# Gated S5 and SiLU mixture on one core: C and three quarters of x turned by transposing transfers

## The chip, the cores and the metric

The kernel runs on one core of a Trainium2 chip. The core has a matrix engine (TensorE, in the profile PE, its weight loads PEld), VectorE (DVE), ScalarE (ACT), GpSimd (POOL) and SyncE (SP), which does nothing here but issue transfers. The engines run side by side, each through its own list of instructions in order, and wait for each other through semaphores. The metric is the device time of one execution in microseconds, the median of some runs.

## The reference

For 2048 tokens x of width 448, two branches are computed and mixed by a gate of each token:

```python
x = A_x
g = _sigmoid((x * gate_w).sum(-1, keepdims=True))
# a: a diagonal complex recurrence (S5) with 448 states
dt = jnp.exp(log_dt)
Lam_bar = jnp.exp(dt * Lam)
B_bar = ((Lam_bar - 1.0) / Lam)[:, None] * Bmat
Bu = jnp.einsum("bld,pd->blp", x + 0j, B_bar)
for t in range(L):
    h = Lam_bar[None, :] * h + Bu[:, t, :]
    hs.append(h)
a = 2.0 * jnp.einsum("blp,dp->bld", hseq, Cmat).real + x * Dskip[None, None, :]
# b: a dense layer pair, width 1792
b = silu(x @ w1) @ w2
out = g * a + (1 - g) * b
```

Inputs and output are bf16.

## The kernel before

The tokens are cut into four chunks of 512 (`tc` 0 to 3) and sixteen blocks of 128 (`tb` 0 to 15). Everything that TensorE contracts over the width 448 needs x with the width on the partitions: that is the tile `xT`, four column groups of 128 (`XCOL` gives where they begin; they overlap) for each chunk. The natural x, with tokens on the partitions, is the tile `xnat`; it is also where the sum of the branches is gathered (`Tb` is another name for it).

For each chunk the work is:

- `x_products` (line 711): the products of `xT` with w1 ("F" tiles, 14 for each chunk) and with the turned B (`BT`, "B" tiles, 7 for each chunk). They run as half-array products of 64 rows, two tiles abreast, in pairs with two PSUM banks. `evict` (line 670) takes a pair out: F tiles through Silu on ScalarE into `aT`, B tiles into `UG`. For chunk 0, `UDVE` lists the B pairs that VectorE evicts; the others go to ScalarE.
- `lanes` (line 754): VectorE rotates `UG` by cosines and sines, runs seven scans of 512 steps (line 784), rotates back and leaves the states in `H`. GpSimd's transfers cast the scan's result to bf16. The products on the way back are written to `PO`; the later half of them has the name `PO1`. Chunk follows chunk, since a scan starts from the end of the one before.
- `gates` (line 897): VectorE multiplies `xnat` by the gate weights into `xg` and by the skip weights in place; ScalarE sums, takes tanh and scales. For chunks after the first it runs after `Gf0`, the first scan of the lanes then under way.
- `ffn2` (line 816, tag G): the product of `aT` with w2; ScalarE scales it into `fe` and a GpSimd transfer adds it into `xnat`.
- `readout` (line 834, tag C): the product of `H` with the readout weights `CP`. The result is scaled and added either by VectorE (line 853, into `ot`, five buffers, then a store), or, for the blocks in `OUTA`, by ScalarE (line 848, into `ct`), an adding transfer of GpSimd (line 850) and a store from `xnat`.

Three things are turned besides. Chunk 0 of x is turned by TensorE at the start (`x0_transposes`). Chunks 1 to 3 are turned by `x_transposes` (line 526): 32 transposes of 64x64 on TensorE into two banks, then two copies into `xT`. B is turned by TensorE (`b_transposes`). C is loaded in its natural form into `Cnat` (a part of `H[2]`; GpSimd clears the rest of it at line 462), turned in 32x32 blocks by VectorE (`readout_columns`, line 870, four instructions into a part of `UG[2]`), and 16 transfers of SP move the blocks to their places in `CP` (line 876). `readout_weights` (line 879) then scales C into `CP` in place: for slots 0 to 2 two ScalarE and two VectorE instructions each, for slot 3, where the real and the imaginary part share the 128 partitions, two half-height ScalarE instructions and one of VectorE.

TensorE's order is the order in which the program adds its work. That of the other engines comes from a planner (`Plan`): each operation has a cost, a priority (a smaller number goes first) and what it reads and writes; the planner plays the run through and sorts by its starting times. The transfers of one queue have rising priorities as they are added (`nl`), so SP's queue keeps the order of the code unless a transfer has to wait. The order is fixed when the program is built: an operation that comes late in the run holds all that the planner put behind it on its engine. `Waits` turns reads and writes by name into semaphore waits. The scaling of C (`CTAT`) is held to 59 us of the plan's time.

The last lines of the body set TensorE's order: F and B of chunks 0 and 1; G of blocks 0 to 3; F of chunk 1, B of chunk 2; G 4 to 7; the rest of F of chunk 2, B of chunk 3, F of chunk 3; C 0 to 7; G 8 to 13; C 8 to 11; G 14 and 15; C 12 to 15.

Of the kernel before, what the change touches and what calls it, by code (L numbers as in the profile page):

```python
# [7 lines left out]
ALU = mybir.AluOpType  # L8
AF = mybir.ActivationFunctionType
# [20 lines left out]
XPRIO = {2: 15, 3: 20.2}  # L30
XBLK = ()
XBEH = {2: "PI_0", 3: "H0_0"}
UDVE = (0, 1, 4, 5, 6)
OUTA = tuple(range(4, 12))
PRMF = (1, 0)
PRMP = 9.7
CPRIO = 2.9
# [3 lines left out]
CBEH = ""  # L41
# [257 lines left out]
def bass_gated_mix__ssm_conv_s5__dense_activation_silu__prompt_kernel(nc, A_x, A_Lambda_re, A_Lambda_im, A_B_re, A_B_im, A_C_re, A_C_im,  # L299
               A_log_dt, A_Dskip, B_x, B_w1, B_w2, gate_w, out):  # L300
    with ExitStack() as ctx:
# [3 lines left out]
        def sb(name, shape, dtype):  # L305
            return E(nc.sbuf_tensor(name, list(shape), dtype))
# [15 lines left out]
        Cnat = H[2][:, :, :].rearrange("p s n -> p (s n)").rearrange("p (b l) -> p b l", b=4)  # L322
        cnn = [f"H2_{s}" for s in range(7)]
# [9 lines left out]
        ot = [sb(f"ot{k}", [128, D_MOD], BF16) for k in range(NOT)]  # L333
        ones = nc.const_aps.tensor(1.0, [128, 512], BF16)
# [53 lines left out]
        def act_cost(n, aps=0):  # L388
            return 0.17 + n * 0.000833 + 0.09 * aps
# [18 lines left out]
        def load(q, dst, src, name, nbytes, prio=None, after=()):  # L408
            nl[0] += 1
            prio = nl[0] if prio is None else prio  # L410
            P.add(q, lambda e: e.dma_start(dst, src), list(after), name.split(), 0.6 if q == "pool" else 0.5 if nbytes > 2000 else 0.35, prio, sem(), nbytes, tag="ld " + name)  # L411
# [36 lines left out]
        def load_xn(tc):
            load("sp", xnat[:, 4 * tc:4 * tc + 4, :],
                 x2[tc * CH:(tc + 1) * CH, :].rearrange("(b p) d -> p b d", p=128), f"xn{tc}", CH * 896)  # L450

        def load_C():

            n = 0
            for b0, b1, p in ((0, 3, 128), (3, 4, 64)):
                rows = lambda a: a[128 * b0:128 * b0 + p * (b1 - b0), :].rearrange("(b p) l -> p b l", p=p)
                for dst, src in (((0, 448), rows(A_C_re)), ((512, 896), rows(A_C_im[:, 0:384])), ((448, 512), rows(A_C_im[:, 384:448]))):
                    load("sp", Cnat[0:p, b0:b1, dst[0]:dst[1]], src, f"Cn{n}" + (" " + " ".join(cnn) if n == 0 else ""),
                         p * (b1 - b0) * max(300, 2 * (dst[1] - dst[0])), None, ["Cnz"] * b0)
                    n += 1  # L460

        POOL(lambda e: e.memset(Cnat[:, 3, :], 0.0), [], ["Cnz"], 0.9, 5)
        load_xn(1)
        load_C()
        load("sp", w2s[:, :, :], B_w2.rearrange("(fb p) d -> p fb d", p=128), "w2", F_FF * 896)
        load_xn(2)
# [55 lines left out]
        for tc in XBLK:  # L522
            xn_of[tc] = {q: [f"xT{tc}_{g}{m}" for g in range(4) for m in range(4)] for q in range(4)}
# [23 lines left out]

        def x_blocks(tc):


            X32 = (xT[:, 3, :, :] if tc == 2 else H[2][:, 0:4, :]).rearrange("p m (q b i) -> p m q b i", q=4, i=32)
            names = [f"XT{tc}2_{k}" for k in range(4)]
            held = cnn if tc == 3 else xn_of[3][0]
            xs = xnat[:, 4 * tc:4 * tc + 4, :]
            for k, (q0, q1, c, b0, b1) in enumerate(((0, 3, 0, 0, 2), (0, 3, 0, 2, 4), (3, 4, XCOL[3], 0, 2), (3, 4, XCOL[3], 2, 4))):
                n = q1 - q0
                src = xs[:, b0:b1, c:c + 128 * n].rearrange("p b (q m i) -> p b q m i", q=n, i=32)
                dst = X32.rearrange("p m q b i -> p b q m i")[:, b0:b1, q0:q1, :, :]
                DVE(lambda e, dst=dst, src=src: e.transpose(dst, src), [f"xn{tc}"] + names[0:k][0:1], [names[k]] + cnn * (tc == 3 and k == 0), 0.15 + 256 * n / 960, XPRIO[tc], "xTd")
            k = sem()  # L560
            for g in range(4):
                for m in range(4):
                    to = xT[32 * m:32 * m + 32, tc, :, :].rearrange("p q (b g i) -> p (q b) g i", b=4, i=32)[:, :, g, :]
                    P.add("sp", lambda e, to=to, g=g, m=m: e.dma_start(to, X32[32 * g:32 * g + 32, m, :, :, :].rearrange("p q b i -> p (q b) i")),
                          names + held, [f"xT{tc}_{g}{m}"], 0.68, 400, k, 150000, tag="xTm")
# [293 lines left out]
        ctn = [f"CT{g}{m}" for g in range(4) for m in range(4)]  # L859

        def readout_columns():

            C32 = UG[2][:, 0:NSLOT, :].rearrange("p s n -> p (s n)").rearrange("p (m t b i) -> p m t b i", m=4, b=4, i=32)
            names = [f"X32_{k}" for k in range(4)]
            held = [f"U2_{s}" for s in range(7)] + ["U2_3i"]
            turned = [f"BT{s}_{h}" for s in range(7) for h in range(2)]
            for b in range(4):
                src = Cnat[:, b, :].rearrange("p (t m i) -> p t m i", m=4, i=32)
                dst = C32.rearrange("p m t b i -> p b t m i")[:, b, :, :, :]
                DVE(lambda e, dst=dst, src=src: e.transpose(dst, src), [f"Cn{n}" for n in range(6)] + ["Cnz"] + [CBEH] * (CBEH != "") + cnn + turned, [names[b]],  # L870
                    0.15 + 896 / 960, CPRIO, "CTd")
            k = sem()
            for g in range(4):
                for m in range(4):
                    to = CP[32 * m:32 * m + 32, :, :].rearrange("p t (b g i) -> p (t b) g i", b=4, i=32)[:, :, g, :]
                    P.add("sp", lambda e, to=to, g=g, m=m: e.dma_start(to, C32[32 * g:32 * g + 32, m, :, :, :].rearrange("p t b i -> p (t b) i")),
                          names + held, [f"CT{g}{m}"], 0.75, 400, k, 300000, tag="CTm")

        def readout_weights(k):

            re, im = CP[:, k, 0:D_MOD], CP[:, 4 + k, 0:D_MOD] if k < 3 else None
            c, cn = ct[k % 2], f"ct{k % 2}"
            both = [cn + "a"]
            if k < 3:
                ACT(lambda e: e.activation(c[:, 0, :], im, AF.Copy, scale=sc2[:, k:k + 1]), ctn + ["sc2"], [cn + "a"], act_cost(448, 1), 8, "ct").at = CTAT
                ACT(lambda e: e.activation(c[:, 1, :], re, AF.Copy, scale=sc2[:, k:k + 1]), ctn + ["sc2"], [cn + "b"], act_cost(448, 1), 8, "ct").at = CTAT
                both.append(cn + "b")
            else:
                for a, b in ((slice(0, 64), slice(64, 128)), (slice(64, 128), slice(0, 64))):
                    ACT(lambda e, a=a, b=b: e.activation(c[a, 0, :], CP[b, 3, 0:D_MOD], AF.Copy, scale=sc2[b, 3:4]), ctn + ["sc2"], [cn + "a"], act_cost(448, 1), 8, "ct").at = CTAT  # L890
            DVE(lambda e: e.scalar_tensor_tensor(re, re, sc1[:, k:k + 1], c[:, 0, :], ALU.mult, ALU.add),
                ctn + ["sc1"] + both, [f"CP{k}"], 0.68, CPP, "CP")
            if k < 3:
                DVE(lambda e: e.scalar_tensor_tensor(im, im, nsc1[:, k:k + 1], c[:, 1, :], ALU.mult, ALU.add),
                    ctn + ["sc1"] + both, [f"CP{4 + k}"], 0.68, CPP, "CP")
# [20 lines left out]
        def xt(tc, who):  # L916
            return [lambda: x_transposes(tc, who)]
# [7 lines left out]
        def C(*tbs):  # L925
# [6 lines left out]
                   {PRMF: [parameters], (K - 2, 0): turn_b[:1], K - 2: turn_b[1:2], K - 1: turn_b[2:], XT1K: xt(1, XT1), 8: [lambda: lanes(0)] + [readout_columns] + [lambda tc=tc: x_blocks(tc) for tc in XBLK]}, [K - 2])  # L932
# [7 lines left out]
        x_products(F(1) + F(2, 0, 1) + B(2), {2: xt(2, "aa")} if 2 not in XBLK else {})  # L940
# [4 lines left out]
        x_products(F(2, 1) + B(3) + F(3), {1: xt(3, "aa") if 3 not in XBLK else [], 9: [lambda: gates(3)]})  # L945
# [40 lines left out]
```

## Time and profile before

| | |
|---|---|
| median of 3 runs | 140.45 us (140.28 to 141.47) |
| the profiled execution | 140.08 us, its span 138.3 us |
| granted TensorE clock | 0.998 |
| busy: PE | 134.7 us (97%) |
| busy: DVE | 119.3 us (86%) |
| busy: ACT | 96.2 us (70%) |
| busy: POOL | 46.4 us (34%) |
| read from memory | 7.11 MB |

All places and lengths come from the profiled execution, whose span begins with its first instruction; the time of a run has some 1.8 us around the span. A line of the order of time gives the start, the length, the engine, the line of the code, the operation, what it writes and reads, and in brackets how long the engine stood idle before it and what ended that. An engine's name with a q (SPq) is its queue of issues. An engine that is busy most of the time is not by that the bound: the chain of waits, followed back from the last instruction, says whose time the kernel takes.

### The profile page before, as it was taken

Reading aid. Unit: us, or ns where it says so; the run is one execution under the profiler, and the core shown is the slowest. Engines: PE = TensorE matmul, PEld = TensorE weight load, DVE = VectorE, ACT = ScalarE, POOL = GpSimd, SP = SyncE. Lnnn points to the kernel's source line nnn. Section 1 sums busy time; section 2 is a strip of 40 time slices with the busy share of each in tenths; the row PEclk is TensorE's granted clock in tenths of the full one; section 3 lists DMA queues with packets and bytes.
Section 4 is the critical chain, followed back from the end, with each engine's and each line's share of the span. In section 5 each row is a group of like instructions: output and inputs, shape, how many; then the busy total and the mean of one; then the engine's idle time right before and its main releaser. Section 6 shows DMA issues by size and latency. Waiting matters only on the chain.

```text
span 138.3 us, 2881 instructions
## 1 busy us (share of the span) xinstructions
PE 134.7 (97%) x1137; PEld 66.0 (48%) x1137; DVE 119.3 (86%) x160; ACT 96.2 (70%) x167; POOL 46.4 (34%) x81
## 2 busy tenths in 40 slices
PE   7999999999999999999999999999999999999991
PEld 2545454445545444455454444445555555555561
DVE  0319999999999999999999999999999999992053
ACT  3259895999647999998299999899643149752200
POOL 7433030300548603067360030724063404374310
PEclk9999999999999999999999999999999999999999
DMA  4999999477859920029654010475459421379542
GB/s 140 324 355 292 270 364 341 63 102 83 96 77 155 158 40 19 24 37 160 93 87 64 0 38 0 65 120 81 114 106 159 102 33 18 51 100 151 118 102 68
DMA packets 33220, 16.48 MB, mean 119 GB/s; under 512 B 17075, under 2 KB 33078, under 8 KB 33206
## 3 DMA queue, kind: packets, MB, share of 16 engines
q0 software_dynamic: 7216, 6.43, 31.6%
q1 hardware_dynamic: 25440, 9.51, 25.8%
q10 hardware_dynamic: 550, 0.36, 0.8%
q8 instruction: 9, 0.15, 0.4%
q14 instruction: 5, 0.04, 0.1%
HBM read 7.11 MB, written 1.84 MB: 65 GB/s over the span
## 4 chain that ended last, share of the span: by engine, by line
PE 96%; DVE 1%; issue 0%; DVEq 0%
PE ps L711 46%; PE ps L822 31%; PE ps L843 14%; PE ps L489 2%; DVE ot L853 1%; PE ps L536 1%; PE ps L504 1%; PE ps L651 1%; PE ps L490 0%; PE ps L583 0%; PE ps L723 0%; DVEq L293 0%
## 5 line engine op out<-in xcount | busy, mean ns | idle before, releaser
L711 PE MATMUL ps<-xT,w1s 64*128 64x512 bf16 x392 | 48.2, 376 | 0.0
L822 PE MATMUL ps<-w2s,aT 128*128 128x448 bf16 x224 | 43.0, 353 | 0.0
L681 ACT ACTIVATE aT<-ps 128x1024 bf16<-128x1024 f32 (+1 forms) x30 | 28.9, 977 | 10.2 <-PE ps L711 10.1
L822 PEld LDWEIGHTS ps<-w2s,aT 128*128 128x128 bf16 x224 | 21.8, 98 | 20.9 <-issue 0.8
L711 PEld LDWEIGHTS ps<-xT,w1s 64*128 64x128 bf16 x392 | 19.6, 94 | 22.5 <-issue 1.2
L711 PE MATMUL ps<-xT,BT 64*128 64x512 bf16 x196 | 25.8, 376 | 0.0
L784 DVE TENSOR_TENSOR_SCAN Gf<-rc,gin,H 128x512 f32<-128x512 f32 x21 | 25.4, 1265 | 0.1
L830 POOL DMA_DIRECT2D xnat<-fe x16 | 14.4, 922 | 31.2 <-ACT fe L828 23.0
L843 PE MATMUL ps<-CP,H 128*128 128x448 bf16 (+2 forms) x126 | 21.7, 332 | 0.0
L411 POOL DMA_DIRECT2D UG<-Gf x27 | 15.7, 660 | 15.7 <-DVE Gf L784 15.4
L828 ACT ACTIVATE fe<-ps,g 128x448 bf16<-128x448 f32 x16 | 9.9, 627 | 11.1 <-PE ps L822 8.1
L843 PEld LDWEIGHTS ps<-CP,H 128*128 128x128 bf16 x126 | 11.6, 98 | 10.0 <-DVE xnat L752 0.4
L711 PEld LDWEIGHTS ps<-xT,BT 64*128 64x128 bf16 x196 | 10.8, 94 | 11.2 <-DVE Gf L609 0.2
L752 DVE TENSOR_TENSOR H<-UG,COS 128x3584 bf16<-128x3584 bf16 (+2 forms) x9 | 16.1, 1810 | 0.0
L411 POOL DMA_DIRECT2D UG<-UG x8 | 4.5, 567 | 27.1 <-ACT UG L690 27.1
L690 ACT ACTIVATE UG<-ps 128x1024 bf16<-128x1024 f32 (+1 forms) x13 | 11.8, 936 | 0.5 <-PE ps L711 0.5
L853 DVE SCALAR_TENSOR_TENSOR ot<-ps,g,xnat 128x448 bf16<-128x448 f32 (+2 forms) x10 | 5.7, 584 | 7.5 <-issue 6.2
L913 ACT ACTIVATE xnat<-xnat,g 128x448 bf16<-128x448 bf16 x16 | 9.7, 663 | 0.1
L906 ACT ACTIVATE junk<-xg 128x448 bf16<-128x448 bf16 x16 | 9.6, 598 | 0.1
L850 POOL DMA_DIRECT2D xnat<-ct x8 | 6.9, 864 | 6.7 <-ACT ct L848 6.6
L848 ACT ACTIVATE ct<-ps,g 128x448 f32<-128x448 f32 x8 | 5.1, 633 | 5.7 <-PE ps L843 5.7
L752 DVE TENSOR_TENSOR PI<-UG,SIN 128x1536 bf16<-128x1536 bf16 (+1 forms) x8 | 8.5, 1083 | 0.0
(99 smaller groups left out, 123.8 us busy)
## 6 DMA issues: line engine op xcount, KB each, us to landing
UG<-Gf POOLq DMA_DIRECT2D x21, 128.0 KB, 2.8
xnat<-fe POOLq DMA_DIRECT2D x16, 112.0 KB, 2.6
w2s<-in_B_w_dram SPq DMA_DIRECT2D x1, 1568.0 KB, 8.5
xnat<-in_A_x_dram SPq DMA_DIRECT2D x3, 448.0 KB, 8.2
CP<-UG SPq DMA_DIRECT2D x16, 56.0 KB, 2.4
xnat<-ct POOLq DMA_DIRECT2D x8, 112.0 KB, 2.9
out_dram<-xnat SPq DMA_DIRECT2D x8, 112.0 KB, 2.3
out_dram<-ot SPq DMA_DIRECT2D x7, 112.0 KB, 1.8
```

What stands on the lines that cost most here:

```text
L411: P.add(q, lambda e: e.dma_start(dst, src), list(after), name.split(), 0.6 if q == "pool" else 0.5 if nbytes > 2000 else 0.35, prio, sem() ...
L681: ACT(lambda e, src=src, dst=dst: e.activation(dst, src(), AF.Silu), [tk, "tbl"], [f"aT{tc % 2}_{m}" for m in names], act_cost(512 * n), 2 ...
L690: ACT(lambda e, src=src, dst=dst: e.activation(dst, src(), AF.Copy), [tk], after, act_cost(512 * n), 5, "U")
L711: r = pe.matmul(bk(toks[k], b), weights(tile, p0, p0 + 64, i), xT[p0:p0 + 64, tc, i, :], start=(h == 0 and n == 0), stop=(h == 1 and n == 2))
L752: DVE(lambda e: e.tensor_tensor(o, a, b, op), r, w, dve_cost(n, 2), prio, tag)
L784: DVE(lambda e, s=s, b=b, init=init: e.tensor_tensor_scan(Gf[:, s, :], rc[:, b:b + 1].to_broadcast([128, CH]), A[:, s, :], init, ALU.mult, ...
L822: r = pe.matmul(bk(tk)[:, 0:D_MOD], aT[tc % 2][:, fb, o:o + 128], w2s[:, fb, :], start=(fb == 0), stop=(fb == NFB - 1))
L828: ACT(lambda e: e.activation(f[:, :], bk(tk)[:, 0:D_MOD], AF.Copy, scale=g1[:, tb:tb + 1]), [tk, f"g1_{tc}"], [fn], act_cost(448, 1), 7, "fe")
L830: P.add("pool", lambda e: e.dma_start(Tb[:, tb, :], f[:, :], accum_op=ALU.add), [fn, f"Tb{tb}"], [f"Tb{tb}"], 0.94, 2, sem(), 250000, tag= ...
L843: r = pe.matmul(bk(tk)[:, 0:b - a], H[tc % 3][:, s, o:o + 128], CP[:, s, a:b], start=(s == 0), stop=(s == NSLOT - 1))
L906: ACT(lambda e, tb=tb, b=b: e.activation(junk[:, :], xg[:, b, :], AF.Copy, accum_out=zl[:, tb:tb + 1]), ["xg"], ["junk", f"zl{tc}"], act_c ...
L913: ACT(lambda e, tb=tb: e.activation(Tb[:, tb, :], xnat[:, tb, :], AF.Copy, scale=g[:, tb:tb + 1]), [f"xd{tc}", f"g_{tc}"], [f"Tb{tb}"], ac ...
```

## The change

Chunks 1, 2 and 3 of x (`XDMA`) are turned by SP's transposing transfers straight from the input into `xT`, two for each chunk: one for three column groups and one for the fourth. C is turned by four such transfers into `CP` and, for the last columns of its imaginary part, into the output buffer `ot[4]` (`C3`). The six loads of C, the memset, VectorE's block transposes and the 16 moves go, as do the 96 TensorE transposes of chunks 1 to 3 and their six copies. SP's queue after the loads of w1: chunk 1 turned, the two rows of gate and skip weights, w2, chunk 2 turned, C turned, then the natural x of chunks 1, 2 and 3. Chunk 3 is turned later: its transfers wait for `PO1` (`XAFT`), as `lanes(0)` writes it. Before, the natural x of chunk 1 was loaded right behind the two rows and ahead of C and w2.

`readout_weights` takes slot 3 apart into two VectorE instructions of half height. `UDVE` gives VectorE all B pairs of chunk 0, and `OUTA` leaves ScalarE the readouts of blocks 8 to 11 alone, so that those of blocks 4 to 7 go through VectorE. Functions that are no longer called (`x_blocks`) are taken out of the code.

```diff
-UDVE = (0, 1, 4, 5, 6)
-OUTA = tuple(range(4, 12))
+XDMA = (1,2,3)
+XAFT = ["PO1"]
+UDVE = (0, 1, 2, 3, 4, 5, 6)
+OUTA = (8, 9, 10, 11)
...
+        C3, c3n = ot[NOT - 1], " ".join(f"ot{NOT - 1}{m}" for m in range(3))
...
+        def turn(dst, src, name, nbytes, cost, after=()):
+
+            nl[0] += 1
+            P.add("sp", lambda e: e.dma_start_transpose(dst, src), list(after), name.split(), cost, nl[0], sem(), nbytes, tag="ldT " + name)
+
+        def turn_x(tc, after=()):
+            for c, n in ((0, 3), (3, 1)):
+                turn(xT[:, tc, c:c + n, :], x2[tc * CH:(tc + 1) * CH, XCOL[c]:XCOL[c] + 128 * n], " ".join(f"xT{tc}_{q}" for q in range(c, c + n)), CH * 256 * n, 2.6 if n == 3 else 1.3, after)
+
+        def turn_C():
+
+
+            for k, a in enumerate((A_C_re, A_C_im)):
+                turn(CP[:, 4 * k:4 * k + 3, 0:D_MOD], a[:, 0:384], " ".join(f"CT{4 * k + m}" for m in range(3)), 448 * 768, 1.5)
+                turn((CP[:, 3, 0:D_MOD], C3[:, :])[k][:, None, :], a[:, 320:448], "CT3" if k == 0 else c3n, 448 * 256, 1.6)
+
+        if 1 in XDMA:
+            turn_x(1)
         for dst, src, name in ((gwb, gate_w, "gwb"), (dkb, A_Dskip, "dkb")):
...
-        POOL(lambda e: e.memset(Cnat[:, 3, :], 0.0), [], ["Cnz"], 0.9, 5)
-        load_xn(1)
-        load_C()
+        if 1 not in XDMA:
+            load_xn(1)
         load("sp", w2s[:, :, :], B_w2.rearrange("(fb p) d -> p fb d", p=128), "w2", F_FF * 896)
+        if 2 in XDMA:
+            turn_x(2)
+        turn_C()
+        if 3 in XDMA and not XAFT:
+            turn_x(3)
+        if 1 in XDMA:
+            load_xn(1)
         load_xn(2)
         load_xn(3)
...
+            up = slice(64, 128)
             if k < 3:
...
+                re, im, rn, mn = CP[:, k, 0:D_MOD], CP[:, 4 + k, 0:D_MOD], f"CT{k}", f"CT{4 + k}"
+                a, to = slice(0, 128), ((CP[:, k, 0:D_MOD], re, sc1, [f"CP{k}", rn], 0), (CP[:, 4 + k, 0:D_MOD], im, nsc1, [f"CP{4 + k}", mn], 1))
             else:
...
+                re, im, rn, mn = CP[up, 3, 0:D_MOD], C3[up, :], "CT3", c3n
+                a, to = up, ((CP[0:64, 3, 0:D_MOD], re, nsc1, ["CP3"], 0), (CP[up, 3, 0:D_MOD], im, sc1, ["CP3", rn], 1))
...
-                   {PRMF: [parameters], (K - 2, 0): turn_b[:1], K - 2: turn_b[1:2], K - 1: turn_b[2:], XT1K: xt(1, XT1), 8: [lambda: lanes(0)] + [readout_columns] + [lambda tc=tc: x_blocks(tc) for tc in XBLK]}, [K - 2])
+                   {PRMF: [parameters], (K - 2, 0): turn_b[:1], K - 2: turn_b[1:2], K - 1: turn_b[2:], XT1K: xt(1, XT1) if 1 not in XDMA else [], 8: [lambda: lanes(0)] + [lambda: turn_x(3, XAFT)] * (3 in XDMA and bool(XAFT))}, [K - 2])
...
-        x_products(F(1) + F(2, 0, 1) + B(2), {2: xt(2, "aa")} if 2 not in XBLK else {})
+        x_products(F(1) + F(2, 0, 1) + B(2), {2: xt(2, "aa")} if 2 not in XDMA else {})
...
-        x_products(F(2, 1) + B(3) + F(3), {1: xt(3, "aa") if 3 not in XBLK else [], 9: [lambda: gates(3)]})
+        x_products(F(2, 1) + B(3) + F(3), {1: xt(3, "aa") if 3 not in XDMA else [], 9: [lambda: gates(3)]})
```

More of the change, by code (lines that the diff above doesn't have):

```diff
@@ L29 @@
 XT1 = "da"
-XPRIO = {2: 15, 3: 20.2}
-XBLK = ()
-XBEH = {2: "PI_0", 3: "H0_0"}
-UDVE = (0, 1, 4, 5, 6)
-OUTA = tuple(range(4, 12))
+XDMA = (1,2,3)
+XAFT = ["PO1"]
+UDVE = (0, 1, 2, 3, 4, 5, 6)
+OUTA = (8, 9, 10, 11)
 PRMF = (1, 0)
 PRMP = 9.7
-CPRIO = 2.9
 CPP = 20.5
@@ L40 @@
 GPR = (14, 20.3, 21.5, 19)
-CBEH = ""
 CASTB = (360000, 360000, 360000)
@@ L321, in bass_gated_mix__ssm_conv_s5__dense_activation_silu__prompt_kernel @@
         H = [sb(f"H{k}", [128, NSLOT, CH], BF16) for k in range(3)]
-        Cnat = H[2][:, :, :].rearrange("p s n -> p (s n)").rearrange("p (b l) -> p b l", b=4)
-        cnn = [f"H2_{s}" for s in range(7)]
         COS = sb("COS", [128, NSLOT, CH], BF16)
@@ L443, in bass_gated_mix__ssm_conv_s5__dense_activation_silu__prompt_kernel, with load_xn @@
         load_w1("sp", len(w1cuts) - 2, 2, 4)
+        def load_xn(tc):
+            load("sp", xnat[:, 4 * tc:4 * tc + 4, :],
+                 x2[tc * CH:(tc + 1) * CH, :].rearrange("(b p) d -> p b d", p=128), f"xn{tc}", CH * 896)
+        def turn(dst, src, name, nbytes, cost, after=()):
[10 more added lines that the diff above has]
+            turn_x(1)
         for dst, src, name in ((gwb, gate_w, "gwb"), (dkb, A_Dskip, "dkb")):
@@ L446, in bass_gated_mix__ssm_conv_s5__dense_activation_silu__prompt_kernel @@
                  name, 128 * 896)
[L448 to L460, printed above, removed]
-        POOL(lambda e: e.memset(Cnat[:, 3, :], 0.0), [], ["Cnz"], 0.9, 5)
-        load_xn(1)
-        load_C()
-        load("sp", w2s[:, :, :], B_w2.rearrange("(fb p) d -> p fb d", p=128), "w2", F_FF * 896)
+        if 1 not in XDMA:
+            load_xn(1)
+        load("sp", w2s[:, :, :], B_w2.rearrange("(fb p) d -> p fb d", p=128), "w2", F_FF * 896)
+        if 2 in XDMA:
[5 more added lines that the diff above has]
+            load_xn(1)
         load_xn(2)
@@ L521, in bass_gated_mix__ssm_conv_s5__dense_activation_silu__prompt_kernel @@
         xn_of = {tc: {q: [f"xT{tc}_{h}" for h in range(2)] for q in range(4)} for tc in range(1, NCH)}
-        for tc in XBLK:
-            xn_of[tc] = {q: [f"xT{tc}_{g}{m}" for g in range(4) for m in range(4)] for q in range(4)}
+        for tc in XDMA:
+            xn_of[tc] = {q: [f"xT{tc}_{q}"] for q in range(4)}
         xn_of[0] = {q: [f"xT0_{q}{part}{h}" for part in range(2) for h in range(2)] for q in range(4)}
@@ L546, in x_transposes @@
                     ACT(lambda e, src=src, dst=dst: e.activation(dst, src(), AF.Copy), [tk], [f"xT{tc}_{h}"], act_cost(1024), 2.2, "xTe")
[L548 to L565, printed above, removed]
         cosn = [f"COS{k}" for k in range(4)] + ["COSd"]
@@ L857, in readout @@
                       [f"ot{tb % NOT}{n}"], [], 0.3, 1, outs[tb % NOT], 128 * 2 * (b - a), tag="st")
[L859 to L877, printed above, removed]
@@ L879, in readout_weights @@
         def readout_weights(k):
-            re, im = CP[:, k, 0:D_MOD], CP[:, 4 + k, 0:D_MOD] if k < 3 else None
             c, cn = ct[k % 2], f"ct{k % 2}"
-            both = [cn + "a"]
+            up = slice(64, 128)
             if k < 3:
-                ACT(lambda e: e.activation(c[:, 0, :], im, AF.Copy, scale=sc2[:, k:k + 1]), ctn + ["sc2"], [cn + "a"], act_cost(448, 1), 8, "ct").at = CTAT
-                ACT(lambda e: e.activation(c[:, 1, :], re, AF.Copy, scale=sc2[:, k:k + 1]), ctn + ["sc2"], [cn + "b"], act_cost(448, 1), 8, "ct").at = CTAT
-                both.append(cn + "b")
-            else:
-                for a, b in ((slice(0, 64), slice(64, 128)), (slice(64, 128), slice(0, 64))):
-                    ACT(lambda e, a=a, b=b: e.activation(c[a, 0, :], CP[b, 3, 0:D_MOD], AF.Copy, scale=sc2[b, 3:4]), ctn + ["sc2"], [cn + "a"], act_cost(448, 1), 8, "ct").at = CTAT
@@ L891, in readout_weights @@
[L891 to L895, printed above, removed]
+                re, im, rn, mn = CP[:, k, 0:D_MOD], CP[:, 4 + k, 0:D_MOD], f"CT{k}", f"CT{4 + k}"
+                a, to = slice(0, 128), ((CP[:, k, 0:D_MOD], re, sc1, [f"CP{k}", rn], 0), (CP[:, 4 + k, 0:D_MOD], im, nsc1, [f"CP{4 + k}", mn], 1))
+            else:
+                re, im, rn, mn = CP[up, 3, 0:D_MOD], C3[up, :], "CT3", c3n
+                a, to = up, ((CP[0:64, 3, 0:D_MOD], re, nsc1, ["CP3"], 0), (CP[up, 3, 0:D_MOD], im, sc1, ["CP3", rn], 1))
@@ new lines, in readout_weights @@
+            ACT(lambda e: e.activation(c[a, 0, :], im, AF.Copy, scale=sc2[a, k:k + 1]), mn.split() + ["sc2"], [cn + "a"], act_cost(448, 1), 8, "ct").at = CTAT
+            ACT(lambda e: e.activation(c[a, 1, :], re, AF.Copy, scale=sc2[a, k:k + 1]), [rn, "sc2"], [cn + "b"], act_cost(448, 1), 8, "ct").at = CTAT
+            for dst, src, f, w, n in to:
+                DVE(lambda e, dst=dst, src=src, f=f, n=n: e.scalar_tensor_tensor(dst, src, f[a, k:k + 1], c[a, n, :], ALU.mult, ALU.add),
+                    ([rn] if n == 0 else mn.split()) + ["sc1", cn + "ab"[n]], w, 0.68, CPP, "CP")
```

## The prediction

> **What bounds the kernel now.** I read the chain of waits in order of time first, because it says which engine's time is the kernel's time.
>
> ```profile
> 13.42 4.53 PE ps L711 x42
> 17.95 0.47 PE ps L536 x32
> 18.41 9.71 PE ps L711 x90
> 28.13 10.70 PE ps L822 x56
> 38.83 5.50 PE ps L711 x50
> 44.33 0.47 PE ps L536 x32
> ...
> 66.72 3.99 PE ps L711 x36
> 70.71 0.47 PE ps L536 x32
> 71.18 21.80 PE ps L711 x202
> ...
> 130.16 3.99 PE ps L843 x21
> 134.15 0.03 issue
> ```
>
> Columns: start, length, what ran. From 0.78 to 134.15 us the chain is TensorE and nothing else, each piece starting where the one before ends. The pieces are also dense: 90 half-array products run two abreast, so 45 slots in 9.71 us, 0.2158 us each, and 202 make 101 slots in 21.80 us, the same. So TensorE waits for nobody after the start, and whatever leaves its queue shortens the run one for one until another engine is late. L536, the transposes of tokens 512 to 2047, stands in the chain three times.
>
> Next came VectorE's order of time, since it is the second busiest engine (119.3 us busy) and feeds TensorE's last stage.
>
> ```profile
> 19.21 0.68 DVE L544 COPY xT<-ps 128x1024 bf16<-128x1024 bf16 x1
> 19.81 1.09 DVE L870 STREAM_TRANSPOSE UG<-H 128x896 bf16<-128x896 bf16 x1
> ...
> 21.41 3.07 DVE L870 STREAM_TRANSPOSE UG<-H 128x896 bf16<-128x896 bf16 x3
> ...
> 45.90 1.07 DVE L752 TENSOR_TENSOR xg<-xnat,gwb 128x1792 bf16<-128x1792 bf16 x1
> ...
> 123.28 2.09 DVE L752 TENSOR_TENSOR H<-H,PO 128x2048 bf16<-128x2048 bf16 x2
> 131.58 0.68 DVE L853 SCALAR_TENSOR_TENSOR ot<-ps,g,xnat 128x448 bf16<-128x448 f32 x1 [6.21 <-issue]
> ```
>
> It is full from about 10 to 125.37 us, then idle 6.21 us. At 125.37 the last H is done, which TensorE takes at 130.16: VectorE is 4.79 us ahead of need at the end, and that is all the slack it has. 45.90 is where it first touches the second chunk of xnat (gates).
>
> Last, SP's queue in order of time, which the change rewrites.
>
> ```profile
> 6.16 1.00 SPq L411 DMA_DIRECT2D w1s<-in_B_w_dram  x2
> ...
> 14.83 0.59 SPq L411 DMA_DIRECT2D w2s<-in_B_w_dram  x1
> 15.47 3.30 SPq L411 DMA_DIRECT2D xnat<-in_A_x_dram  x2
> 24.51 12.23 SPq L876 DMA_DIRECT2D CP<-UG  x16
> ```
>
> The queue is idle after 36.7 us until the stores at 96.6. The last w1 loads are issued by 7.16 and land 5.9 us later (the list of DMA issues), so about 13.0; w2 lands 8.5 us after 14.83, at 23.3, and is needed at 28.13.
>
> **The change part by part.** *TensorE.* Three groups of 32 transposes go: 3 x 0.47 = 1.41 us, all of it in the chain. The pieces behind them lose nothing more, since 9.71 and 21.80 us are already the bare slots.
>
> *ScalarE.* Five copies of L546 (1.02 each), one eviction of a U pair (1.03) and four of L848 (0.633) go: 8.7 us less. It is 70% busy; worth nothing by itself.
>
> *VectorE.* Gone: four L870 transposes, 4 x 1.077 = 4.31, and one L544 copy, 0.68. Added: the U pair that UDVE gives it, 1.21 (the other two L688 casts of that shape); the outputs of blocks 4 to 7, 4 x 0.677 = 2.71 (L853); and one more L891-like operation for slot 3, 0.67. Sum -4.99 + 4.59 = -0.40. Up to 45 us only the first two and the U pair count, so VectorE reaches the second chunk's gates 3.8 us earlier, at about 42.1; it gives that back later. It is then done with the last H near 125.0, and TensorE wants it at 130.16 - 1.41 = 128.75: 3.8 us of slack remain. The added outputs sit among lanes' operations of at most 2.03 us; a PSUM bank is held that much longer, and there are eight, of which the readouts fill one per 1.34 us.
>
> *GpSimd.* Four L850 issues and the 0.84 us memset go; 34% busy, nothing.
>
> *SP's queue and the transfers.* Six C loads and 16 CP moves go; six transposing transfers for x (0.52 MB for each 512 tokens) and four for C (0.92 MB) come. The order after the last w1 load becomes: x's second chunk, gate rows, w2, third chunk, C, then the natural x of all later chunks. The wait that is added, the fourth chunk behind PO1, stands at VectorE's 48.66 less some 3.8 us; behind it on SP are only the stores, first at 96.6, and TensorE wants that chunk at 75 us. It costs nothing unless the transfer takes over 25 us.
>
> The trace shows no transposing transfer. The nearest rows are the plain loads, up to 355 GB/s in the slices of the page (1.5 us for 0.52 MB), and the 16 CP moves in short pieces, 0.92 MB in 12.23 us, 75 GB/s (7.0 us). Faster than a plain load has no reason; slower than the 64-byte pieces is possible, so the bound below stays soft. Call T the time for one x chunk; C takes 1.75 T. I take T = 3.5 us (150 GB/s, twice the CP row's pace and under half the load's): the rows read here are 256 or 768 bytes long, between the 64 bytes of a CP piece and the 896 of a plain load. The Trainium skill, DMA: Bandwidth & Descriptors, section "Latency and other measured facts", gives 261 GB/s for a DMA transpose with a non-contiguous middle dimension; by it T would be 2.0 us and the sum the same. No run here shows it yet.
>
> Landing times, with w1 at 13.0 and the plain bytes at 330 GB/s (the page's slices there run from 270 to 364): second chunk 13.0 + T = 16.5; gate rows and w2 (1.83 MB, 5.6 us) 18.6 + T = 22.1; third chunk 25.6; C 31.7; natural x of the second chunk (1.4 us) 20.0 + 3.75 T = 33.1. Needs: second chunk at 20.8 (TensorE's first product on it, now about 21.3, less 0.47); w2 at 27.7; third chunk at about 48; C after 59, where the CP work is held; natural x at 42.1. Every one is early, so I cost these moves at nothing. What that rests on: second chunk T under 7.8, w2 T under 9.1, natural x 20.0 + 3.75 T under 42.1 + 3.8 = 45.9, T under 6.9 us. The last is the tightest, and it falls about on the CP row's pace.
>
> Sum: -1.41 us. The profiled execution took 140.08 us with a span of 138.3 and 1.8 around it; it would be 138.67 with a span of 136.9. The median shown is 140.45, 0.37 above the profiled one; less 1.41 it is 139.04. The tail, 4.1 us from the last product to the last store, is untouched.
>
> **The rivals.** *A: the transposing transfers are slow, and VectorE's queue waits for natural x.* The order on VectorE is fixed when the program is built. If T is over 6.9 us, xg of the second chunk is at the head and holds the lanes behind it; H of the last chunk is late, and TensorE waits before its last readouts. Price: 3.75 us per us of T beyond 6.9. At T = 8.2 (64 GB/s) it is 4.9 us, so 139.0 + 4.9 = 143.9, and TensorE loses 0.4 at the second chunk as well, which lies inside that. For: 75 GB/s is a row of this very kernel, and the fixed order leaves no way round. Against: those pieces are a quarter as long. A harsher form is a transfer turned block by block. The 16 blocks of a chunk, one after another at even half the median landing of a CP move (2.4 us), make T 19 us, and TensorE stands from 20.8 to 32 us; natural x lands at 91 and the run ends past 180. The Trainium skill, VectorE: DVE Perf Modes, section "The three transpose paths", speaks for this side: 1309 ns for a 128x128 block by the DMA path against 390 on TensorE; were its figure a rate and not the latency of one block, T would be 21 us. In this trace TensorE takes 0.47 us for a whole chunk. Chance of A 0.18.
>
> *B: the 1.41 us is partly given back.* A readout's bank is not free because VectorE, in one of its 2.03 us operations, evicts blocks 4 to 7 late; or VectorE stands behind a TensorE that is later than planned. For: ScalarE did these four within 0.7 us of each product. Against: eight banks, and blocks 0 to 3 go that way now without a gap in the chain. One such wait of up to 1 us leaves 139.5 to 140.0. Chance 0.10.
>
> *C: VectorE becomes the bound at the end* without any late transfer: it needs 3.8 us of new stalls against a balance of -0.40; chance 0.02, time over 139.
>
> That the change doesn't do what it says I leave out: the transposes of all three chunks leave TensorE's order by the diff.
>
> **How the numbers follow.** The sum as it stands has 0.70: 139.0 us, with 138.6 to 139.5 of its own. The 1.41 us is 1.00% of 140.45, right on the bound of 1% that a measurement of this kernel can tell from no change. A run-to-run spread of some tenths (140.28 to 140.45 for two of the three) decides the side, so I halve this case, with a little more for faster since the missing transposes cannot cost less than nothing and ScalarE is relieved: 0.40 faster, 0.30 same. B's 0.10 is same. A's 0.18 is slower, C's 0.02 too. So faster 0.40, same 0.40, slower 0.20. The range runs from 138.6, the sum with its spread, to 143.0, which takes in B and the mild half of A and leaves out its tail, about 0.15, and a little below.
>
> **What would show it.** Right: no L536 in the chain; the chain TensorE from 0.8 to about 132.7; the first product on w2 at about 27.7; VectorE idle for some 4 us before its last outputs. Wrong: an idle stretch of TensorE near 20.8 (second chunk late) or 27.7 (w2 late); idle time of VectorE before xg near 42 (A), with the last readouts following it; a gap in the chain between 92 and 104 (B). The number to read first is the time from issue to landing of an x transposing transfer: under 7 us the sum stands.

## The result, and the profile after

| | before | after |
|---|---|---|
| median | 140.33 us (140.22 to 141.47, 6 runs) | 139.06 us (138.84 to 139.41, 6 runs) |
| profiled execution, its span | 140.08 us, 138.3 us | 139.01 us, 137.2 us |
| busy: PE, DVE | 134.7, 119.3 us | 133.7, 119.4 us |
| busy: ACT, POOL | 96.2, 46.4 us | 88.6, 42.6 us |
| read from memory | 7.11 MB | 6.31 MB |

The ratio is 0.990 (0.987 to 0.9931): 1.27 us less at the median, where 1.41 was forecast. Ratios here are made from undisturbed runs alone; for kernels whose own runs lie far apart, median and range of all runs stand in place of a ratio.

The chain of waits of the changed kernel (start, length, what ran):

```profile
9.01 0.18 PE ps L573 x4
...
13.79 14.24 PE ps L701 x132
28.03 10.70 PE ps L812 x56
38.73 16.73 PE ps L701 x154
55.45 10.70 PE ps L812 x56
66.15 25.79 PE ps L701 x238
91.95 10.70 PE ps L833 x56
...
129.13 5.35 PE ps L833 x42
...
```

and of the kernel before, at the small products with the parameters:

```profile
8.64 0.18 PE ps L583 x4
```

In the changed kernel it is still TensorE from the start to the last product. The three pieces of 0.47 us are gone and their neighbours have joined: 14.24 = 4.53 + 9.71, 16.73 = 5.50 + 11.22 and 25.79 = 3.99 + 21.80, to a hundredth. The last readouts start at 129.13 instead of 130.16, only 1.03 us earlier, because this execution was 0.37 us late from its start: 13.79 for 13.42, and already 9.01 for 8.64 at the products with the parameters (L573, before L583), before any changed work. From that point to the last readouts it is 120.12 us for 121.52: 1.40 us less. I use this distance below, since it leaves the start out. The last piece holds all 42 readout products here and 21 before, because the chain before goes over to VectorE's outputs half way; the products are the same.

SP's queue in order of time:

```profile
7.20 5.43 SPq L447 DMA_TRANSPOSE xT<-in_A_x_dram  x2
12.68 0.58 SPq L407 DMA_DIRECT2D gwb<-in_gate_w_dram  x1
...
14.51 0.44 SPq L407 DMA_DIRECT2D w2s<-in_B_w_dram  x1
15.00 9.52 SPq L447 DMA_TRANSPOSE xT<-in_A_x_dram  x2
24.56 3.57 SPq L447 DMA_TRANSPOSE CP<-in_A_C_re_dram  x2
...
31.11 3.84 SPq L407 DMA_DIRECT2D xnat<-in_A_x_dram  x3
47.80 2.77 SPq L447 DMA_TRANSPOSE xT<-in_A_x_dram  x2
```

The second column is time on the queue, and here lies what the plain loads did not show: behind other traffic a pair of transposing transfers holds the queue for 9.52 us, and everything after it is issued that much later. On an empty queue (47.80) a pair takes 2.77.

VectorE in order of time, where it first touches the natural x of the second chunk, and at the end:

```profile
42.88 1.07 DVE L742 TENSOR_TENSOR xg<-xnat,gwb 128x1792 bf16<-128x1792 bf16 x1
...
124.04 2.09 DVE L742 TENSOR_TENSOR H<-H,PO 128x2048 bf16<-128x2048 bf16 x2
130.55 0.68 DVE L843 SCALAR_TENSOR_TENSOR ot<-ps,g,xnat 128x448 bf16<-128x448 f32 x1 [4.41 <-issue]
```

It reaches xg at 42.88 without a wait (45.90 before), and has the last H at 126.13, 3.0 us ahead of need.

### The profile page after: what moved, and what is told of

Read it like the earlier page. It is cut to its first block, busy times and chain, and to the rows that moved or that the text cites. A ratio compares the mean times of both kernels' runs of the same rounds, so it can differ in the third digit from the quotient of the medians.

```text
span 137.2 us, 2658 instructions
## 1 busy us (share of the span) xinstructions
PE 133.7 (97%) x1041; PEld 64.9 (47%) x1041; DVE 119.4 (87%) x161; ACT 88.6 (65%) x157; POOL 42.6 (31%) x76
## 3 DMA queue, kind: packets, MB, share of 16 engines
HBM read 6.31 MB, written 1.84 MB: 59 GB/s over the span
## 4 chain that ended last, share of the span: by engine, by line
PE 97%; DVE 0%; issue 0%
PE ps L701 47%; PE ps L812 31%; PE ps L833 16%; PE ps L498 2%; PE ps L513 1%; PE ps L641 1%; DVE ot L843 0%; PE ps L713 0%; PE ps L499 0%; PE ps L573 0%
## 5 line engine op out<-in xcount | busy, mean ns | idle before, releaser
L701 PEld LDWEIGHTS ps<-xT,w1s 64*128 64x128 bf16 x392 | 20.2, 95 | 23.1 <-issue 0.8
L818 ACT ACTIVATE fe<-ps,g 128x448 bf16<-128x448 f32 x16 | 10.1, 630 | 20.5 <-PE ps L812 16.6
L742 DVE TENSOR_TENSOR H<-UG,COS 128x3584 bf16<-128x3584 bf16 (+2 forms) x9 | 16.2, 1814 | 0.0
L843 DVE SCALAR_TENSOR_TENSOR ot<-ps,g,xnat 128x448 bf16<-128x448 f32 (+2 forms) x14 | 8.2, 614 | 5.7 <-issue 4.4
L680 ACT ACTIVATE UG<-ps 128x1024 bf16<-128x1024 f32 (+1 forms) x12 | 10.6, 920 | 0.0
L742 DVE TENSOR_TENSOR PO<-UG,SIN 128x1536 bf16<-128x1536 bf16 (+1 forms) x8 | 8.6, 1086 | 0.2 <-DMA UG<-Gf 0.2
L742 DVE TENSOR_TENSOR H<-H,PI 128x3584 bf16<-128x3584 bf16 x4 | 8.1, 2022 | 0.1
```

Of the source, the lines that this page charges most:

```text
L680: ACT(lambda e, src=src, dst=dst: e.activation(dst, src(), AF.Copy), [tk], after, act_cost(512 * n), 5, "U")
L701: r = pe.matmul(bk(toks[k], b), weights(tile, p0, p0 + 64, i), xT[p0:p0 + 64, tc, i, :], start=(h == 0 and n == 0), stop=(h == 1 and n == 2))
L742: DVE(lambda e: e.tensor_tensor(o, a, b, op), r, w, dve_cost(n, 2), prio, tag)
L818: ACT(lambda e: e.activation(f[:, :], bk(tk)[:, 0:D_MOD], AF.Copy, scale=g1[:, tb:tb + 1]), [tk, f"g1_{tc}"], [fn], act_cost(448, 1), 7, "fe")
```

## The experiments

Each kernel differs from the changed one, or from the kernel before, by the edit shown; all compute the whole result. "Before" is always the kernel before on the same chip.

**C alone, and one chunk of x.** The first kernel keeps C's transfers and the two lists (`UDVE` and `OUTA`), and turns x on TensorE as before. The second turns x's second chunk by transfers as well.

```diff
-XDMA = (1,2,3)
+XDMA = ()
```

> C is turned by transposing transfers as in the changed kernel; all of x goes back to TensorE's transposes. Theory (the whole gain is the 3 x 0.47 us that leave TensorE's queue): 140.4 us, that is 139.06 + 1.41, within 0.3 of the kernel before, with L-number of the transposes three times in the chain. Rival (the gain comes from the C path, that is from the 16 moves and VectorE's block transposes that go): about 139.1 us, as the changed kernel.

140.20 us (12 runs), before 140.37; ratio 0.9992 (0.9977 to 1.0007). Its chain:

```profile
17.98 0.47 PE ps L545 x32
...
44.36 0.47 PE ps L545 x32
...
70.74 0.47 PE ps L545 x32
```

All three pieces are back. Turning C takes 4 us of VectorE's work, the memset and 16 moves away, and with the two lists but without x that is worth nothing.

```diff
-XDMA = (1,2,3)
+XDMA = (1,)
```

> Only the second chunk of x and C are turned by transfers, the third and fourth chunk by TensorE. Theory: one third of the gain, 139.06 + 0.94 = 140.0 us. Rival (the gain is not in TensorE's transposes but in C or in the evictions given to other engines): 139.1. A second rival (the first chunk's transfer pays for something late at the start, the others not): 140.4 or more.

139.92 us (12 runs), before 140.37; ratio 0.9972 (0.9948 to 0.9996). From the parameter products to the last readouts it takes 121.52 us before, 121.52 with C alone, 121.05 with one chunk and 120.12 with three: 0.47 less for one chunk, 0.93 for the other two. The gain goes by the chunk, in the size of the row.

**The changed kernel once more, unaltered,** on another chip, for the 0.37 us of the start.

> The changed kernel once more, unaltered, beside the others of this call. Expected 139.0 to 139.1 us. In its first profile TensorE's first products were 0.37 us later at 9.0 us than in the kernel before, ahead of anything that the change touches but the queue behind the last w1 load. If that is chance, the profile here has TensorE's first tile of parameters between 8.6 and 8.8 and a span near 136.9; if it belongs to the change (the transposing transfers slow the last w1 loads), it is at 9.0 again.

139.07 us (12 runs), before 140.47; ratio 0.9906 (0.9867 to 0.9945), 1.40 us less. The parameter products come at 8.96, late again, which the expectation had taken as a sign of the change. The trace says otherwise: the first products wait for a load of w1 issued at 2.25 and landed at 6.28, ahead of SP's first transposing transfer at 7.20, and the kernel with x alone (below), whose queue issues the same transfers up to there (the first transposing one at 7.26), has them at 8.51. Across the profiles here those products begin between 8.5 and 10.4 us, and in the four where they come last, from 10.0 us on, w1's two loads of 256 KB land late (in 5.4 to 5.8 us, 4.0 before). In the first profile of the changed kernel they land in 4.0 too, so its own 0.37 us stays unexplained. A single profile can thus be off by more than the effect.

**VectorE's and ScalarE's lists.** Three kernels put both lists back, or one.

```diff
-UDVE = (0, 1, 2, 3, 4, 5, 6)
-OUTA = (8, 9, 10, 11)
+UDVE = (0, 1, 4, 5, 6)
+OUTA = tuple(range(4, 12))
```

> The changed kernel with UDVE and OUTA as before: ScalarE evicts one more U pair and the readouts of blocks 4 to 7. Theory (ScalarE and VectorE both have slack, so who evicts is worth nothing): 139.1 us, within 0.3 of the changed kernel, VectorE idle about 2.5 us longer before its last outputs. Rival (the shift of evictions is part of the gain, by banks that come free sooner): 139.6 or more.

139.48 us (11 runs), before 140.37; ratio 0.9942 (0.991 to 0.9973), so 0.4 us worse than expected. The next two kernels take the lines of that diff one at a time, first `OUTA`, then `UDVE`.

> The changed kernel with OUTA alone as before (ScalarE and adding transfers bring out blocks 4 to 7). With both settings as before the time was 139.48 us against 139.06 and 139.07 of the changed kernel, though TensorE's chain was as long. Theory (the 0.4 us come from the output path, adding transfers and stores in place of VectorE): 139.4 to 139.6 us. Rival (it was UDVE, or chance): 139.0 to 139.2.

> The changed kernel with UDVE alone as before (ScalarE evicts the second U pair of the first chunk). Theory (the early eviction is hidden behind TensorE either way): 139.0 to 139.2 us. Rival (the 0.4 us come from here): 139.4 to 139.6, with TensorE's chain longer before 30 us.

OUTA as before: 139.63 us (12 runs), before 140.38; ratio 0.9949 (0.9909 to 0.9988). UDVE as before: 139.18 us (12 runs), before 140.38; ratio 0.9916 (0.9882 to 0.995), as the changed kernel within the intervals. So it is OUTA. From the start of the last readouts to the end of the span it is 8.07 us in the changed kernel (137.2 - 129.13) and 8.04 with the old UDVE, but 8.63 with both lists old and 8.65 with the old OUTA: some 0.55 us lie in the tail, after the bound has done its work. VectorE's last output ends 5.72 us after the start of the last readouts in all four, so the 0.55 us lie in the stores behind it. With both lists old SP's last wait, for a store to land, shows them; here it is first in the changed kernel, then with both lists old:

```profile
SPq L924 <- DMA out_dram<-ot: 0.9, 1, 0.9
```

```profile
SPq L924 <- DMA out_dram<-ot: 1.5, 1, 1.5
```

Why the stores land later is not shown. The kernel before has the old OUTA too and a tail of 8.14 us, so the new list gains nothing against it; it is the old list together with the change that goes badly. The three kernels below that turn x but keep C's old path have the old OUTA and tails of 8.15 to 8.33 us, so it seems to take C's new path as well. The intervals of the ratios overlap, and the tails, of one profile each, are the firmer evidence.

**x alone.** Here the kernel before gets the turned x, while C is loaded and turned as before, behind the transfers. The third chunk's transfers and the natural x stand as in the changed kernel, and the fourth chunk waits for `PO1`; the lists are the old ones.

```diff
+        turn_x(1)
         for dst, src, name in ((gwb, gate_w, "gwb"), (dkb, A_Dskip, "dkb")):
...
-        load_xn(1)
-        load_C()
         load("sp", w2s[:, :, :], B_w2.rearrange("(fb p) d -> p fb d", p=128), "w2", F_FF * 896)
+        turn_x(2)
+        load_C()
+        load_xn(1)
...
```

> The kernel before with the transposing transfers of x alone; C keeps its loads, VectorE's block transposes and the 16 moves, and the natural x of the second chunk comes behind C. Theory: the same 1.41 us off, 139.0 us, since C's path hangs on no wait of TensorE. Rival (C's path has to go for the gain to show, because its loads and moves meet x's transfers): 139.7 or more, with idle time of VectorE before the second chunk's gates or of TensorE near 21 or 28 us.

Six runs from 139.56 to 146.82 us, median 144.6; before 140.37. The same three pieces are out of TensorE's queue and the median is 4 us longer; one run of the six came to 139.56, where the whole change is. What differs between the runs is not shown, since one execution was traced. The chain of waits of that one, of 145.34 us, says how the time is lost there:

```profile
14.87 6.34 SPq L448
21.25 1.45 SPq L448
...
26.12 4.50 DMA H<-in_A_C_im_dram
...
31.78 3.05 DVE UG L882 x3
...
43.92 6.65 DVE Gf L796 x6
50.57 0.99 DVE xg L764
51.58 0.67 ACT junk L918 x2
52.25 0.92 ACT aT L693
53.17 0.05 issue
53.22 8.16 PE ps L723 x48
```

The third chunk's pair holds SP's queue for 7.8 us; C's loads are issued behind it and the last lands at 30.6. VectorE has C's block transposes next in its fixed order and stands for 5.17 us. It carries the delay through its scans to xg (50.48, where it was 45.90), ScalarE's sums wait for xg, and a Silu eviction stands behind them on ScalarE: TensorE finds no free bank for 3.38 us. The windows show the rest (stretch, PE busy and products, granted clock, DMA share, GB/s):

```profile
48.00:52.00 4.00, 1.83 (x18) 1.00 1.14 152
52.00:54.00 2.00, 0.78 (x4) 0.53 1.08 143
54.00:58.00 4.00, 4.00 (x22) 0.50 0.79 123
58.00:62.00 4.00, 4.00 (x32) 0.88 0.31 65
```

After the gap the clock is halved for some six us, and 48 products that make 24 slots of 0.2158 us, 5.18 us, take 8.16. The gap and this make 3.38 + 2.98 = 6.36 us; by the distance from the parameter products to the last readouts the loss against the changed kernel is 6.36.

Two kernels aim at VectorE's wait. The first issues C's loads ahead of w2, the second keeps the loads and plans the block transposes for 29 us.

```diff
+        load_C()
         load("sp", w2s[:, :, :], B_w2.rearrange("(fb p) d -> p fb d", p=128), "w2", F_FF * 896)
         turn_x(2)
-        load_C()
```

> The kernel with x's transposing transfers alone and C in its old way, but C's loads ahead of w2 and of the third chunk's transfers. Theory (x alone lost its gain because C's loads stood behind 0.5 MB of transposing transfers and w2, and VectorE's block transposes of C wait at a fixed place): VectorE waits little for C, no gap in TensorE, 139.0 to 139.4 us. Rival (the 16 moves and the block transposes themselves collide with the transfers, wherever the loads stand): a gap in TensorE between 40 and 60 us again and 142 us or more.

Ten runs from 139.48 to 144.35 us, median 141.06; before 140.47, so neither the 139.0 to 139.4 us nor the 142 that were expected. In the run of 144.35 us, the slowest of the ten, VectorE still stands for 4.37 us before the block transposes at 23.89. C's last load, issued at about 17.8 and 5.8 us on its way, lands at 23.6; the profile names a Silu eviction that ends at 23.78 as the last to release it, so the two can't be told apart here. A cast of U stands behind on VectorE, and TensorE waits for it:

```profile
25.63 1.56 PE L723 MATMUL ps<-xT,BT 64*128 64x512 bf16 x9 [2.92 <-DVE UG L700]
26.57 0.63 PE L723 MATMUL ps<-xT,w1s 64*128 64x512 bf16 x1
```

A product that took 0.38 us takes 0.63 after it: the clock fell after 2.92 us too (0.61 and 0.54 in the next two stretches of 2 us), and the 48 products that make 5.18 us take 7.04.

```diff
                     0.15 + 896 / 960, CPRIO, "CTd")
+                    0.15 + 896 / 960, CPRIO, "CTd").at = 29.0
```

> The kernel with x's transposing transfers alone (C in its old way, loaded behind them), with one thing changed in VectorE's order: the four block transposes of C stand behind the first three operations of the lanes and not ahead of them; all other engines' orders are the same. Theory (x alone lost its gain because VectorE stood 5.2 us at the block transposes waiting for C's loads with the lanes behind them): the wait shrinks to 1 to 1.5 us, VectorE reaches the second chunk's gates near 46.5 us and not at 50.5, the 3.4 us gap of TensorE goes, and the time is 139.0 to 140.0 us. Rival (the transfers and the 16 moves disturb each other, whoever waits): 142 us or more as before.

Eleven runs from 139.62 to 142.28 us, median 140.57; before 140.53. The block transposes start at 31.09 without a wait, the long gap and the slow clock are gone, 4 us of the median are won back, and still nothing is gained where 139.0 to 140.0 was expected. The chain of a run of 142.25 us now ends its detour in the 16 moves:

```profile
53.41 1.60 SPq L888
55.05 2.31 DMA CP<-UG
57.44 0.61 ACT UG L702
58.09 10.77 PE ps L834 x56
```

They took 20.5 us of SP's queue (12.2 in the kernel before), and they read from the tile that the third chunk's U needs: ScalarE's eviction into `UG` waits 3.80 us for them, and TensorE 1.42. By the distance from the parameter products to the last readouts this run takes 121.60 us, 121.52 before and 120.12 in the changed kernel, so this gap takes the gain away. So with C's old path x's gain shows in single runs (139.48 to 139.62 us at best), not at the median. The parts are not worth alone what they are worth together: nothing for C, nothing or a loss for x, 1.4 us for both.

**How much slack there is.** Seven transposing transfers that nobody needs (3.75 times a chunk's, into parts of `UG[2]` and `H[2]`) are put on SP's queue between C and the natural x; every other engine keeps its order.

```diff
+            if o.tag == "ld xn1":
+                for dst, names in ((UG[2][:, 0:3, :], "U2_0 U2_1 U2_2"), (UG[2][:, 3:4, :], "U2_3 U2_3i"), (UG[2][:, 4:7, :], "U2_4 U2_5 U2_6"), (UG[2][:, 7:8, :], "U2_7a U2_7b"),
+                                   (H[2][:, 0:3, :], "H2_0 H2_1 H2_2"), (H[2][:, 3:4, :], "H2_3"), (H[2][:, 4:7, :], "H2_4 H2_5 H2_6")):
+                    turn(dst, x2[CH:2 * CH, 0:128 * dst.shape[1]], names, 0, 0.0)
+                    W.put(P.ops[-1])
```

> The changed kernel with seven more transposing transfers (3.75 chunks of x into tiles that are free then, read by nobody) on SP's queue ahead of the natural x of the second chunk; every engine's order is otherwise the same. It should land near 36.7 + 3.75 x 3.5 = 49.8 us instead of 36.7, and VectorE reach the second chunk's gates 6.9 us late. The prediction's account (the loss shows at the end, when the last H is late, beyond 3.0 us of slack): 139.06 + 3.9 = 143.0 us, a gap of TensorE near 130 us. Account from the run of x alone (ScalarE waits for xg in its fixed order with Silu evictions behind it, banks run out and TensorE stops near 48 us, and runs at a lower granted clock for some us after): 143.5 to 145 us, a gap of 2 to 4 us near 48 to 52 us and none at the end. If the natural x has more margin than both say: 139.1.

Four runs from 143.56 to 149.22 us, median 147.3, longer than either account had it; before 140.47. Only the fastest, of 143.56 us, was traced. Its VectorE:

```profile
46.35 1.09 DVE L742 TENSOR_TENSOR xg<-xnat,gwb 128x1792 bf16<-128x1792 bf16 x1 [2.35 <-DMA xnat<-in_A_x_dram]
...
51.99 0.96 DVE L742 TENSOR_TENSOR PO<-UG,SIN 128x1536 bf16<-128x1536 bf16 x1 [1.89 <-DMA UG<-Gf]
```

and TensorE, in order of time:

```profile
72.45 4.71 PE L701 MATMUL ps<-xT,w1s 64*128 64x512 bf16 x42 [1.26 <-ACT fe L818]
78.90 0.37 PE L701 MATMUL ps<-xT,w1s 64*128 64x512 bf16 x1 [1.74 <-issue]
```

VectorE is held twice, by the natural x and by a cast of a scan's result. The chain goes through the cast, which took 7.58 us to land (44.29 to 51.87; the median of such casts is 2.7), so VectorE would have stood for a cast landing then even with the natural x in time. That transposing transfers slow those of other queues is not shown by it: between 44 and 52 us only 144 of 2488 packets are under 512 bytes, where from 28 to 41 us, with the extra transfers, 7508 of 7798 are. Beside the cast run the plain loads of all the natural x, issued from 41.23 us on, where the extra transfers had pushed them. With 1.04 us of a late start taken off, VectorE is 4.1 us later at 51.99 than in the changed kernel (46.81), and TensorE loses 3.50: the two gaps and 0.50 in refilling (4.71 + 17.59 us for the 202 products that take 21.80 in one piece). So all but some 0.6 us of VectorE's lateness is paid. It is paid at 72 and 78 us, not at the last readouts, where the last H comes at 131.3, 2.4 us ahead of need, and not near 50 us as with x alone. The first gap comes by GpSimd's queue. A cast there that needs VectorE's scan is issued at 67.22 us (62.04 in the changed kernel), an adding transfer of `fe` stands behind it, and ScalarE's next eviction into `fe` waits until that has landed:

```profile
67.22 0.52 POOL UG L407
67.74 3.94 DMA xnat<-fe
...
71.76 0.64 ACT fe L818
```

The way to the second gap is ScalarE's sums, which in the changed kernel already wait at this place:

```profile
72.04 0.58 ACT L874 ACTIVATE junk<-xg 128x448 bf16<-128x448 bf16 x1 [0.82 <-DVE xg L742]
72.52 0.19 ACT L874 ACTIVATION_READ_ACCUMULATOR junk<-xg 128x1 f32 x1
72.62 1.00 ACT L671 ACTIVATE aT<-ps 128x1024 bf16<-128x1024 f32 x1
```

The sum of the next gates stands 0.82 us for VectorE, with a Silu eviction behind it. TensorE still has banks there; with the delay ScalarE's wait grows to 3.00 us at 77.22, and it has none. Before the change ScalarE had no such wait there.

**One step further: B turned by transfers too.** B's loads and TensorE's transposes go for six transposing transfers, and chunk 0's F tiles run first.

```diff
-        x_products(F(0, 0, NH) + B(0) + F(0, NH) + B(1),
+        x_products(F(0) + B(0) + B(1),
...
+        for src, c0, c1, r in ((A_B_re[0:448, :], 0, 448, "r"), (A_B_im[384:448, :], 448, 512, "3"), (A_B_im[0:384, :], 512, 896, "i")):
+            for i0, n, c in ((0, 3, 0), (3, 1, 320)):
+                turn(BT[:, i0:i0 + n, c0:c1], src[:, c:c + 128 * n], f"BT{r}{i0}", 256 * n * (c1 - c0), 1.5)
```

> The same idea for B: its two matrices are turned by six transposing transfers behind all of w1, the 56 transposes of B leave TensorE (0.23 + 0.23 + 0.35 = 0.81 us of the chain), and TensorE does all of the first chunk's w1 products ahead of the B products, to give the transfers time. Theory: 139.06 - 0.81 = 138.25 us if B lands by 16 us. Rival: B or the second chunk of x, which is now behind it, lands late: an idle stretch of TensorE at 16 or 20 us, with a lower granted clock after it, and 139 us or more.

140.39 us (12 runs), before 140.47; ratio 0.9986 (0.9951 to 1.0021). VectorE and TensorE:

```profile
22.20 1.09 DVE L740 TENSOR_TENSOR xg<-xnat,gwb 128x1792 bf16<-128x1792 bf16 x1 [2.24 <-DMA gwb<-in_gate_w_dram]
```

```profile
24.49 3.84 PE L699 MATMUL ps<-xT,BT 64*128 64x512 bf16 x34 [1.33 <-DVE UG L676]
```

The gate row was issued at 17.63 instead of 12.68, VectorE stands for it with U's casts behind, and TensorE pays. This execution, of 139.62 us, is the fastest of the twelve; what the others lose beyond it is not shown. The next kernel issues the two rows from ScalarE's queue.

```diff
-            load("sp", dst[:, :], src.rearrange("(o n) -> o n", o=1).partition_broadcast(128).rearrange("p o n -> p (o n)"),
-                 name, 128 * 896)
+            row = src.rearrange("(o n) -> o n", o=1).partition_broadcast(128).rearrange("p o n -> p (o n)")
+            P.add("act", lambda e, dst=dst, row=row: e.dma_start(dst[:, :], row), [], [name], 0.5, 20, sem(), 128 * 896, tag="ld " + name).at = 5.3
```

> B turned by transposing transfers as in the run before, but the gate and skip rows are issued on ScalarE's queue near 5 us and no longer on SP's behind all of B. There, VectorE stood 2.2 us waiting for the gate row with U evictions behind it and TensorE lost 1.33 us at 23 us. Theory: that gap goes and TensorE's 0.81 us show: 138.3 us, 138.0 to 138.6. Rival (the transfers of B push another load behind its need as soon as this one is out of the way): a gap elsewhere and 139 us or more.

Twelve runs from 138.29 to 142.51 us, median 140.9; before 140.53. TensorE in a run of 140.88 us:

```profile
11.75 4.71 PE L699 MATMUL ps<-xT,w1s 64*128 64x512 bf16 x42 [0.49 <-DVE phk L559]
...
21.59 6.87 PE L699 MATMUL ps<-xT,BT 64*128 64x512 bf16 x62 [0.54 <-DMA xT<-in_A_x_dram]
29.07 5.09 PE L810 MATMUL ps<-w2s,aT 128*128 128x448 bf16 x26 [0.61 <-DMA w2s<-in_B_w_dram]
```

The wait for the row is gone; now the second chunk and w2 land late, each by half a us, and TensorE waits as long for VectorE's work on the parameters (`phk`). One run of twelve came to 138.29; the kernel as a whole does not beat the change.

## Why the prediction was right, and where its steps were not

**TensorE's term** was right: 1.41 us forecast, 1.40 in the chain, 0.47 for the chunk tried alone, and nothing moved in to fill it. The forecast of 139.0 us met a median of 139.06. Of rivals B and C nothing shows: TensorE has no gap between 92 and 104 us, and the last H is in time.

**Transfers hidden, T = 3.5 us**: right. w1's last load lands near 12.8 and the second chunk near 16.2; w2 lands at 24.6 and the third chunk at 28.0: 3.4 us each for 0.52 MB, about 150 GB/s. These are distances between landings; the third chunk's first transfer was issued at 15.00, beside w2. C took some 4.7 us for 0.92 MB, 195 GB/s, 1.4 T and not 1.75. The Trainium skill, DMA: Bandwidth & Descriptors, section "Latency and other measured facts", has 261 GB/s for a DMA transpose with a non-contiguous middle dimension; both measurements are below it. The Trainium skill, VectorE: DVE Perf Modes, section "The three transpose paths", has 1309 ns for one 128x128 block; 16 blocks land here in 3.4 us, 0.21 us a block, so that figure is not the rate of a long transfer, and the harsh form of rival A falls.

**Landing times** were mis-sized, each on the safe side of its need. The gate rows and w2 took some 8.4 us and not 5.6: w2 came at 24.6 for 22.1, and was needed at 28.0. The natural x came at about 36.7 for 33.1, and was needed at 42.9. The sign to be read first, under 7 us from issue to landing for a transfer of x, was a poor one: the six took 4.6 to 13.0 us and the sum stood. The 13.0 is that of the third chunk's first, issued at 15.00 behind w2, which itself landed at 24.6.

**VectorE's balance** was forecast as -0.40 us and is +0.1; xg came at 42.88 for 42.1, the last H at 126.13 for 125.0, its idle time ahead of the last outputs is 4.41 us. Slack at the last readouts is 3.0 and not 3.8 us. TensorE paid for none of that.

**ScalarE's, VectorE's and GpSimd's parts costed at nothing**: right against the kernel before (C alone 0.9992; the old UDVE as good as the new; tail 8.07 for 8.14 us), though ScalarE is relieved by 7.6 us and not by 8.7. That the old OUTA would cost 0.5 us in the changed kernel's tail was not foreseen, and its cause stays open.

**Rival A** was placed wrong, though the outcome did not hang on it. It took the last readouts as the point where a late VectorE is paid, with 3.8 us free until then. The run with the late natural x shows two others, at 72 and 78 us, where ScalarE's evictions stand behind an adding transfer held up by a cast and behind the next chunk's sums, both waiting for VectorE, and a margin of some 0.6 us. So the step "VectorE is 4.79 us ahead of need at the end, and that is all the slack it has" failed: it is the slack at one of several places, and not the least. The wait it named, for the natural x, was there (2.35 us) but was not the one that ended last; a cast's was. "What that rests on: T under 6.9 us" is by that too generous, by how much no run with a slower T shows.

**Adding parts up** was harmless here only because the parts came together. By the sum, x alone should have kept the 1.41 us; it lost 4 at the median, and in the traced run it lost 6.36 against the changed kernel through C's loads behind the transposing transfers on SP's queue.

## What to carry to other kernels

When work leaves the bounding engine for a queue of transfers, count what stands behind it on that queue by time on the queue (2.8 us for an idle pair, 9.5 behind traffic), and whether another engine's fixed order meets a late load. Look for an engine's slack at each place where another waits for it, among them evictions that stand behind its results on a third engine, and not at the last use alone. Try a change's parts in pairs before one is called useless: C turned by transfers is worth nothing alone, and without it x's gain is gone at the median.

## What the runs showed of the hardware

- The granted clock: gaps of 3.38 and 2.92 us on TensorE were followed by 0.50 to 0.61 for four to six us and products of 0.63 us instead of 0.38, and so cost 6.36 and 4.78 us (2.92 and the 1.86 by which 7.04 is over 5.18). Gaps of 1.26, 1.33, 1.42 and 1.74 us left it at 1.00. The Trainium skill, TensorE: Matmul & The Clock Gate, section "Why this matters for your kernels", warns of gaps over about 3 us; these rows agree, and here the mark lies somewhere between 1.74 and 2.92.
- While the fourth chunk was being turned (49 to 51 us) the DMA engines show a share of 2.04 at 144 GB/s, where plain loads (17 to 21 us before the change) show 1.07 at 358. That share cannot be read as a load when transposing transfers are in it.
